# A mixture-of-experts stage: one copy moved to another engine, a group of transposes issued later, two slots exchanged

## The chip, the cores and the metric

The kernel runs on one core of a Trainium2 chip. The metric is the device time of one execution in microseconds (us), the median of several runs. TensorE (PE in the rows) multiplies matrices into the eight PSUM banks; ScalarE (ACT) and VectorE (DVE) copy results out of PSUM and convert data; GpSimd (POOL) issues the gathers and scattered stores, SyncE (SP) the loads of weights. Each engine works through its own instruction list in the order of the program, and waits on semaphores for the others.

## What is computed

Attention with capped scores, a dense layer with a normalisation, and then a routed layer: each of 1792 tokens is sent to one of 8 experts, and the expert's two weight matrices are applied with a ReLU between them. The change lies in this last layer:

```python
def _moe2_ref(x, modality_id, w_gate, modality_bias, w1, w2):
    logits = x @ w_gate + modality_bias[modality_id]
    e_idx = np.argmax(logits, axis=1)
    ...
    for e in range(E):
        mask = e_idx == e
        if not mask.any():
            continue
        h = np.maximum(x[mask] @ w1[e], 0.0)          # 768 -> 1024
        out[mask] = gate_w[mask, None] * (h @ w2[e])  # 1024 -> 768
```

## The kernel before

Attention, the dense layer and the routing fill the first 545 us. Then two tiles of tokens of an early expert (names with `e_`) are finished, and the tokens that are left go through *slots* of fixed size in the order of `STATIC`, each with one expert's weights: kind D holds 512 tokens, F 256, H 128. The order before is D0, H0, D1, H1, F0. Two small slots of 32 tokens (kind T) ride along, T0 with D0 and T1 with D1 (`SMALL`). The gathered rows of tokens are `yg`.

For each slot the program writes the same stages, and the order in which `run_slots` writes them is the order in which every engine does them:

- `s_tr` of the *next* slot: TensorE transposes its token tiles, six 128x128 blocks a tile, into PSUM (`xt`), three blocks to a half; ScalarE copies each half to `xh`, VectorE writes what the rounding left over to `xl`.
- `s_h` (D, F) or `s_hh` (H): the first matrix. The accumulators are `ph`: eight PSUM banks for D, four for F, two for H. Each product is made of three matmuls, high by high, high by low and low by high. For D and F, ScalarE's ReLU gives `hh` and VectorE's remainder `hl`. For H the result lies the other way round, so ScalarE writes `hu`, `s_ht` transposes it (`ht`), and then come `hh` and `hl`.
- `s_o`: the second matrix, accumulators `po`, eight blocks of weights (f = 0 to 7). `store` scales the result into `ob` (half on ScalarE, half on VectorE), and GpSimd scatters it to the output. The last slot does its tiles one after the other.
- A T slot has its own stages: `t_tr` (rows of the small slot are scaled on VectorE, transposed into `tp`, copied to `tx` on ScalarE), `t_h` (`th`, ReLU to `tu`), `t_ht` (transposed into `tt`, copied to `hT`), `t_o` (`to`, copied to `tb`). In lines L1191 to L1193 the copy of `tt` to `hT` is VectorE's:

```python
        pt = ctile(f"tt{sname(s)}")[:, :NC1]
        ...
        dve.tensor_copy(h, pt)
```

All of these PSUM tiles come from one pool of eight banks (`ctile`): a new tile takes the bank that was given back longest ago, and its first matmul waits until that bank's last reader is done.

Weights arrive by `c_load` (SyncE loads a block into one of four `raw` buffers) and `c_split` (ScalarE casts it to `wh`, L1025; VectorE writes `wl`, L1026, which gives the raw buffer back). Six blocks of 512 KB belong to a slot's first matrix, eight of 384 KB to its second. They go into two rings of buffers, 12 and 16 tiles, so that a block can be split only when the block that had its place is used up. `step`, called ahead of each block of matmuls, writes the splits that this block needs and up to `QUOTA` = 2 more. So splits stand in ScalarE's and VectorE's lists between the copies of the slots.

Of the kernel before, what the change touches and what calls it, by code (L numbers as in the profile page):

```python
# [15 lines left out]
ALU = mybir.AluOpType  # L16
# [4 lines left out]
B, H, S, D = 4, 12, 448, 64  # L21
NT, DM, DF, NE = 1792, 768, 1024, 8
# [4 lines left out]
NF = DF // P  # L27
# [15 lines left out]
TAIL = (12, 12, 10)  # L43
NS = NK * len(KINDS)
NG = COL0["T"]
STATIC = [("D", 0), ("H", 0), ("D", 1), ("H", 1), ("F", 0)]
SMALL = {0: ("T", 0), 2: ("T", 1)}
PLAIN = 3
DIRECT = 6
# [41 lines left out]
def attn_moe_kernel(ctx, tc, qt, kt, vv, cap, w_in, w_out, g_ln, ids, w_gate, mbias, w1, w2, out):  # L91
    nc = tc.nc
    pe, act, dve, pool, sp = nc.tensor, nc.scalar, nc.vector, nc.gpsimd, nc.sync
# [5 lines left out]

    keys = ["rest", ("E", 0), ("E", 1)] + [(x, i) for x in STATIC + list(SMALL.values()) for i in range(UNIT[x[0]])]  # L100
    oviews = dict(zip(keys, dram_disjoint_views(out, len(keys))))

    def oview(s, i):
        return oviews.get((s, i), oviews["rest"])
# [83 lines left out]
    def route_consts(tp):  # L188
# [39 lines left out]
        for i, kind in enumerate(KINDS):  # L228
            pool.memset(ck[:, i:i + 1], float(COL0[kind]))
            there = [x for x in STATIC + list(SMALL.values()) if x[0] == kind]  # L230
            pool.memset(own[:, i:i + 1], float(UNIT[kind] * len(there)))
# [623 lines left out]
    t = (B - 1) * S // P - 1  # L855
# [101 lines left out]
    while msteps or due:  # L957
        if msteps:
            msteps.pop(0)[1]()
        if outs and outs[-1] in groups:  # L960
            g = outs[-1]
# [22 lines left out]
    ss = {}  # L984
    NC1, NC2 = DF // 4, DM // 4

    def ctile(nm):
        return late["ps"].tile([P, 512], F32, tag="C", name=nm)

    def sname(s):  # L990
        return f"{s[0]}{s[1]}"

    def cols(s):
        kind, i = s
        return [COL0[kind] + UNIT[kind] * i + x for x in range(UNIT[kind])]
# [41 lines left out]
            gs.append(g)  # L1037
        ss[s] = {"g": gs, "ga": ga}

    def s_tr(s, part=range(4)):  # L1040
        nm = sname(s)
        n = len(cols(s))
        if 0 in part:
            ss[s]["xh"] = g2.tile([P, ND, n * P], F32R, tag="xh2", name=f"xh2_{nm}")
            ss[s]["xl"] = g2.tile([P, ND, n * P], F32R, tag="xl2", name=f"xl2_{nm}")
        xh, xl, ga = ss[s]["xh"], ss[s]["xl"], ss[s]["ga"]
        for i in range(n):
            if i not in part:
                continue
            g = ss[s]["g"][i]  # L1050
            o = slice(i * P, (i + 1) * P)
            for q in range(2):
                pt = ctile(f"xt{nm}_{i}_{q}").rearrange("p (b c) -> p b c", c=P)
                r = slice(3 * q, 3 * q + 3)
                for d in range(3):
                    pe.transpose(pt[:, d, :], g[:, (3 * q + d) * P:(3 * q + d + 1) * P], ident)
                act.copy(xh[:, r, o], pt[:, :3, :])
                dve.tensor_sub(xl[:, r, o], pt[:, :3, :], xh[:, r, o])
            dve.tensor_scalar(ga[:, i:i + 1], g[:, DM:DM + 1], 1e-9, None, op0=ALU.add)
        if n - 1 in part:  # L1060
            dve.reciprocal(ga[:, :n], ga[:, :n])

    def s_h(s, step):
# [53 lines left out]
            dve.tensor_sub(hl[:, c, :], pt, hh[:, c, :])  # L1117
        ss[s]["hh"], ss[s]["hl"] = hh, hl

    def s_o(s, step, last):  # L1120

        nm = sname(s)
        hh, hl, ga = ss[s]["hh"], ss[s]["hl"], ss[s]["ga"]
        cs = cols(s)
        pos = [[ctile(f"po{nm}_{i}_{hf}") for hf in range(2)] for i in range(len(cs))]
        ws = {}

        def store(i):
            ob = g2.tile([P, DM], F32, tag="tm", name=f"ob{nm}_{i}", bufs=NTM)
            act.activation(ob[:, :HD], pos[i][0][:, :HD], AF.Copy, scale=ga[:, i:i + 1])  # L1130
            dve.tensor_scalar(ob[:, HD:], pos[i][1][:, :HD], ga[:, i:i + 1], None, op0=ALU.mult)
            pool.indirect_dma_start(out=oview(s, i), out_offset=IndirectOffsetOnAxis(ap=sidx[:, cs[i]:cs[i] + 1], axis=0),
                                    in_=ob, in_offset=None, bounds_check=NT, oob_is_err=False)

        for group in [[i] for i in range(len(cs))] if last else [list(range(len(cs)))]:
            for f in range(NF):
                if f not in ws:
                    step(s, 1, f)
                    ws[f] = ss.pop((s, 1, f))
                wh, wl = ws[f]  # L1140
                for i in group:
                    o = slice(i * P, (i + 1) * P)
                    for hf in range(2):
                        c = slice(hf * HD, (hf + 1) * HD)
                        p = pos[i][hf][:, :HD]
                        pe.matmul(p, hh[:, f, o], wh[:, c], start=(f == 0), stop=False)  # L1146
                        pe.matmul(p, hh[:, f, o], wl[:, c], start=False, stop=False)  # L1147
                        pe.matmul(p, hl[:, f, o], wh[:, c], start=False, stop=(f == NF - 1))  # L1148
                    if f == NF - 1:
                        store(i)  # L1150
# [3 lines left out]
    def t_gather(s):  # L1154
        g = g2.tile([P, YW], F32, tag="gT", name=f"yg{sname(s)}")[:TT]
        pool.indirect_dma_start(out=g, out_offset=None, in_=ysc,
                                in_offset=IndirectOffsetOnAxis(ap=gidxT[:TT, s[1]:s[1] + 1], axis=0),
                                bounds_check=NT, oob_is_err=False)
        ga = g2.tile([TT, 1], F32, tag="gt", name=f"gt{sname(s)}", bufs=2)
        ss[s] = {"g": g, "ga": ga}  # L1160

    def t_tr(s):
        g, ga = ss[s]["g"], ss[s]["ga"]
        dve.tensor_scalar(ga, g[:, DM:DM + 1], 1e-9, None, op0=ALU.add)
        dve.reciprocal(ga, ga)
        dve.tensor_scalar(g[:, :DM], g[:, :DM], ga, None, op0=ALU.mult)
        x = g2.tile([P, DM], F32, tag="tm", name=f"tx{sname(s)}", bufs=NTM)[:, :ND * TT].rearrange("p (b c) -> p b c", c=TT)
        pt = ctile(f"tp{sname(s)}")[:, :ND * TT].rearrange("p (b c) -> p b c", c=TT)
        for d in range(ND):
            pe.transpose(pt[:, d, :], g[:, d * P:(d + 1) * P], ident[:TT, :TT])  # L1170
        act.copy(x, pt)
        ss[s]["x"] = x
# [14 lines left out]
    def t_ht(s):  # L1187
        u = ss[s]["u"]
        pt = ctile(f"tt{sname(s)}")[:, :NC1]
        for b in range(NC1 // P):  # L1190
            pe.transpose(pt[:, b * P:(b + 1) * P], u[:, b * P:(b + 1) * P], ident)  # L1191
        h = g2.tile([P, DM], F32, tag="tm", name=f"hT{sname(s)}", bufs=NTM)[:, :NC1]
        dve.tensor_copy(h, pt)  # L1193
        ss[s]["h"] = h

    def t_o(s, step):
# [15 lines left out]
    def run_slots(seq, small, lead=None):  # L1212

        smalls = [small[n] for n in sorted(small)]
        use = []
        for n, s in enumerate(seq):
            t = [small[n]] if n in small else []
# [42 lines left out]

        if seq[0][0] == "T":
            t_gather(seq[0])
            t_tr(seq[0])
            t_h(seq[0], step)
            t_ht(seq[0])
            t_o(seq[0], step)
            return

        def first(i):
            if i < len(cols(seq[0])):  # L1270
                s_tr(seq[0], (i,))
            elif smalls:
                t_tr(smalls[0])
                if smalls[1:]:
                    t_gather(smalls[1])
# [13 lines left out]
        for n, s in enumerate(seq):  # L1289
            nx = seq[n + 1] if n + 1 < len(seq) else None  # L1290
            t, tn = small.get(n), small.get(n + 1)
            (s_hh if s[0] == "H" else s_h)(s, step)
            if t:
                t_h(t, step)
            if s[0] != "H":
                if nx:
                    s_tr(nx)
            else:
                if nx:
                    s_tr(nx, (0,))  # L1300
                s_ht(s)
                if nx:
                    s_tr(nx, (1, 2, 3))
            if t:
                t_ht(t)
            if tn:
                t_tr(tn)
                for x in smalls[smalls.index(tn) + 1:][:1]:
                    t_gather(x)
            if n + 2 < len(seq):  # L1310
                s_gather(seq[n + 2])
            if t:
                t_o(t, step)
            s_o(s, step, n == len(seq) - 1)

    def lead(advance, tr):

# [13 lines left out]
    with tc.manual_schedule():  # L1331
        run_slots(STATIC, SMALL, lead)

# [3 lines left out]
    def rest(kind, n, i):  # L1337
        if i == MAXS[kind]:
            return
        with tc.If(n > UNIT[kind] * i):  # L1340
            if kind == "T":
                run_slots([(kind, i)], {0: (kind, i)})
            else:
                run_slots([(kind, i)], {})
            rest(kind, n, i + 1)

    with tc.If(more > 0):
        for i, kind in enumerate(KINDS):
            n = nc.values_load(nsl[0:1, i:i + 1], min_val=0, max_val=UNIT[kind] * NK)
            rest(kind, n, len([x for x in STATIC + list(SMALL.values()) if x[0] == kind]))  # L1350
    for pl_ in (late["ps"], late["g1"], g2, g3, g4):
# [40 lines left out]
```

## Time and profile before

| | |
|---|---|
| median of 3 runs | 815.36 us (812.24 to 815.41) |
| the profiled execution: its own time | 816.4 us |
| its span, first to last instruction | 814.6 us |
| TensorE busy, share of the span | 95% |
| mean granted TensorE clock | 0.97 |

The profile is of one execution, which is 1.0 us above the median. A row of a timeline gives start, duration, engine, line, operation, output and inputs, the count of merged instructions and, in brackets, the engine's idle time before it with what ended it. Durations of consecutive matmuls overlap, so that their cost is the distance of their starts.

### The profile page before, as it was taken

The numbers are of one execution on the slowest core, as the hardware profiler recorded it, in microseconds if no ns is written. First come the engines' busy times: TensorE is split into PE (matmuls) and PEld (weight loads), VectorE is DVE, ScalarE is ACT, GpSimd is POOL, SyncE is SP. The second block draws the span as 40 slices with busy tenths as digits, with TensorE's granted clock in tenths as the row PEclk, the third lists the DMA queues.
The fourth block names the chain that finished last, engine by engine and source line by source line (L and its number), as shares of the span: only waits on it lengthen the run. The fifth ranks groups of instructions, "written<-read, shape, count | busy, mean of one in ns | idle before, by whom it ended". The sixth has DMA issues, their size and how long they took to land.

```text
span 814.6 us, 11543 instructions
## 1 busy us (share of the span) xinstructions
PE 770.6 (95%) x4158; PEld 593.0 (73%) x4158; DVE 478.4 (59%) x843; ACT 389.8 (48%) x539; POOL 260.1 (32%) x325
## 2 busy tenths in 40 slices
PE   7888989999999999999999999899999989999983
PEld 2324545676677877577769799799879978799982
DVE  4999897757764566675435755756146171461730
ACT  5665853766755545656651224434144252442530
POOL 3763244544443342438623213441200101001000
PEclk9979979999999999999999999999999989999997
DMA  7866532123322222223000302467928259382711
GB/s 187 253 190 188 175 110 55 47 76 99 97 70 65 77 57 76 88 63 94 12 20 20 138 20 97 153 229 245 387 81 258 104 201 394 130 259 103 239 66 42
DMA packets 41206, 107.28 MB, mean 132 GB/s; under 512 B 7047, under 2 KB 18833, under 8 KB 41138
## 3 DMA queue, kind: packets, MB, share of 16 engines
q1 hardware_dynamic: 34610, 77.01, 29.8%
q0 software_dynamic: 6528, 29.42, 10.4%
q8 instruction: 35, 0.57, 0.3%
q14 instruction: 33, 0.27, 0.1%
HBM read 95.33 MB, written 11.27 MB: 131 GB/s over the span
## 4 chain that ended last, share of the span: by engine, by line
PE 79%; DVE 9%; DMA 5%; issue 3%; ACT 2%; SPq 1%; POOL 0%; POOLq 0%; DVEq 0%; ACTq 0%
PE av L710 8%; PE h L540 5%; PE y L590 5%; PE h L542 5%; PE y L591 5%; PE h L541 5%; PE y L592 5%; PE sc L684 4%; PE sc L686 4%; PE poD L1146 3%; PE poD L1148 3%; PE poD L1147 3%; PE phD L1080 3%; PE phD L1081 3%; PE phD L1079 3%
## 5 line engine op out<-in xcount | busy, mean ns | idle before, releaser
L688 ACT ACTIVATE e<-sc,sc 112x896 f32<-112x896 f32 x96 | 95.8, 1005 | 81.9 <-PE sc L686 67.5
L689 ACT ACTIVATE e<-e,cap_t 112x896 f32<-112x896 f32 x96 | 99.1, 1043 | 1.2
L710 PE MATMUL av<-e,v 112*64 112x448 f32 x384 | 97.4, 577 | 1.9 <-ACT e L689 1.0
L590 PE MATMUL y<-wouh,lh 128*128 128x388 f32 x224 | 77.6, 346 | 1.8 <-ACT lh L580 1.8
L592 PE MATMUL y<-wouh,ll 128*128 128x388 f32 x224 | 76.1, 340 | 0.3 <-DVE ll L581 0.2
L591 PE MATMUL y<-woul,lh 128*128 128x388 f32 x224 | 76.0, 339 | 0.0
L540 PE MATMUL h<-winh,xh 128*128 128x512 f32 x168 | 69.4, 413 | 0.2
L684 PE MATMUL sc<-qs,kh 128*112 128x448 f32 x168 | 64.7, 385 | 4.3 <-DVE qs L668 3.0
L542 PE MATMUL h<-winh,xl 128*128 128x512 f32 x168 | 66.7, 397 | 0.2 <-DVE xl L528 0.2
L541 PE MATMUL h<-winl,xh 128*128 128x512 f32 x168 | 66.3, 395 | 0.0
L686 PE MATMUL sc<-qs,kl 128*112 128x448 f32 x168 | 62.8, 374 | 0.0
L710 PEld LDWEIGHTS av<-e,v 112*64 112x64 f32 x384 | 26.3, 140 | 45.9 <-issue 36.5
L699 POOL TENSOR_TENSOR es<-es,et 112x448 f32<-112x448 f32 x36 | 45.4, 1263 | 28.0 <-DVE et L698 27.1
L669 POOL TENSOR_TENSOR kl<-kr,kh 128x448 fp32r<-128x448 f32 x28 | 34.5, 1232 | 52.8 <-PE sc L686 20.1
L590 PEld LDWEIGHTS y<-wouh,lh 128*128 128x128 f32 x224 | 42.1, 188 | 12.1 <-issue 7.9
L1026 DVE TENSOR_TENSOR wl_H<-raw_H,wh_H 128x768 fp32r<-128x768 f32 (+1 forms) x28 | 29.1, 1070 | 36.9 <-ACT wh_H L1025 36.9
L540 PEld LDWEIGHTS h<-winh,xh 128*128 128x128 f32 x168 | 31.6, 188 | 18.9 <-issue 10.7
L1026 DVE TENSOR_TENSOR wl_D<-raw_D,wh_D 128x768 fp32r<-128x768 f32 (+1 forms) x28 | 29.9, 1071 | 24.9 <-ACT wh_D L1025 23.5
L668 DVE TENSOR_TENSOR qs<-qr,qs 64x448 fp32r<-64x448 f32 x42 | 39.2, 934 | 6.5 <-ACT qs L667 5.3
L1146 PE MATMUL poD<-wh_D,hhD 128*128 128x384 f32 x128 | 43.0, 336 | 0.0
L1148 PE MATMUL poD<-wh_D,hlD 128*128 128x384 f32 x128 | 42.8, 334 | 0.0
L1147 PE MATMUL poD<-wl_D,hhD 128*128 128x384 f32 x128 | 42.8, 334 | 0.0
(392 smaller groups left out, 1811.5 us busy)
## 6 DMA issues: line engine op xcount, KB each, us to landing
kr<-in_kt_dram SPq DMA_DIRECT2D x92, 112.0 KB, 2.5
qr<-in_qt_dram SPq DMA_DIRECT2D x88, 112.0 KB, 2.9
rawi<-in_w_in_dram POOLq DMA_DIRECT2D x12, 512.0 KB, 4.8
rawo<-in_w_out_dram POOLq DMA_DIRECT2D x16, 384.0 KB, 4.0
raw_D<-in_w_dram SPq DMA_DIRECT2D x12, 512.0 KB, 3.6
wr_T<-in_w_dram SPq DMA_DIRECT2D x16, 384.0 KB, 4.1
raw_D<-in_w_dram SPq DMA_DIRECT2D x16, 384.0 KB, 4.8
wr_T<-in_w_dram SPq DMA_DIRECT2D x12, 512.0 KB
```

The source lines that it names most:

```text
L540: pe.matmul(o, s["xh"][d], winh[d][:, c], start=(d == 0), stop=False)
L541: pe.matmul(o, s["xh"][d], winl[d][:, c], start=False, stop=False)
L542: pe.matmul(o, s["xl"][d], winh[d][:, c], start=False, stop=(d == ND - 1))
L590: pe.matmul(o, s["lh"][f], wouh[f][:, c], start=(f == 0), stop=False)
L591: pe.matmul(o, s["lh"][f], woul[f][:, c], start=False, stop=False)
L592: pe.matmul(o, s["ll"][f], wouh[f][:, c], start=False, stop=(f == NF - 1))
L684: pe.matmul(ps[:CK, c, :S], kh[:, k0:k0 + CK], qs, start=True, stop=plain(b, p))
L686: pe.matmul(ps[:CK, c, :S], kl[:, k0:k0 + CK], qs, start=False, stop=True)
L688: act.activation(e, ps[:CK, :, :S], AF.Tanh, scale=sc8[:CK])
L689: act.activation(e, e, AF.Exp, scale=cap_t[:CK])
L710: pe.matmul(o[64 * j:64 * j + 64, :S], v[:, 2 * cp + c, 64 * j:64 * j + 64], et[b, p, j, cp][:, c, :], start=(cp == 0 and c == 0), stop=(c ...
L1146: pe.matmul(p, hh[:, f, o], wh[:, c], start=(f == 0), stop=False)
```

## The change

Three edits. The copy of `tt` to `hT` goes from VectorE to ScalarE, and in the D slots `t_ht` is written between the two halves of the next slot's first tile. `t_tr` is split: the scaling (`t_sc`, VectorE) stays where it was, and the transposes and their copy, which for T1 stood ahead of H0's second matrix, are written inside it, ahead of its block f = 5. And F0 comes before H1.

```diff
-STATIC = [("D", 0), ("H", 0), ("D", 1), ("H", 1), ("F", 0)]
+STATIC = [("D", 0), ("H", 0), ("D", 1), ("F", 0), ("H", 1)]
...
-    def s_tr(s, part=range(4)):
+    def s_tr(s, part=range(4), halves=(0, 1)):
...
-            for q in range(2):
+            for q in halves:
...
-    def s_o(s, step, last):
+    def s_o(s, step, last, late_=None):
...
             for f in range(NF):
+                if f == NF - 3 and late_:
+                    late_()
                 if f not in ws:
                     step(s, 1, f)
...
-    def t_tr(s):
+    def t_sc(s):
         g, ga = ss[s]["g"], ss[s]["ga"]
         dve.tensor_scalar(ga, g[:, DM:DM + 1], 1e-9, None, op0=ALU.add)
         dve.reciprocal(ga, ga)
         dve.tensor_scalar(g[:, :DM], g[:, :DM], ga, None, op0=ALU.mult)
+
+    def t_tr(s):
+        g = ss[s]["g"]
...
-        dve.tensor_copy(h, pt)
+        act.copy(h, pt)
...
-            if s[0] != "H":
-                if nx:
-                    s_tr(nx)
-            else:
+            if s[0] == "H":
                 if nx:
                     s_tr(nx, (0,))
                 s_ht(s)
                 if nx:
                     s_tr(nx, (1, 2, 3))
-            if t:
+            elif t:
+                s_tr(nx, (0,), (0,))
                 t_ht(t)
+                s_tr(nx, (0,), (1,))
+                s_tr(nx, (1, 2, 3))
+            elif nx:
+                s_tr(nx)
             if tn:
-                t_tr(tn)
+                t_sc(tn)
...
-            s_o(s, step, n == len(seq) - 1)
+            s_o(s, step, n == len(seq) - 1, (lambda: t_tr(tn)) if tn else None)
```

**Place 1, slot H0.** TensorE's list from the last transposes of D1's tokens (`xtD1`) to H0's second matrix (`poH0`), and further on the first matmul of three of D1's eight accumulators (`phD1`). What a row waits for stands in brackets (Activation is ScalarE). Before:

```order
L1056 MATMUL xtD1_3_1_6039<-ident_61,ygD1_3_5585 128x128 x2
L1170 MATMUL tpT1_6051<-ident_61,ygT1_5228 128x32 [waits DMASW1_49,DVE_49,PE_49]
L1170 MATMUL tpT1_6051<-ident_61,ygT1_5228 128x32 x5
L1146 MATMUL poH0_0_0_6064<-wh1_H0_0_5787,hhH0_5991 128x384 [waits PE_49,Activation_49]
...
L1079 MATMUL phD1_5_6180<-xh2_D1_5976,wh0_D1_0_6101 128x512 [waits PE_49]
L1079 MATMUL phD1_6_6181<-xh2_D1_5976,wh0_D1_0_6101 128x512 [waits Activation_49]
L1079 MATMUL phD1_7_6182<-xh2_D1_5976,wh0_D1_0_6101 128x512 [waits DVE_49]
```

Of the change:

```order
L1056 MATMUL xtD1_3_1_6039<-ident_61,ygD1_3_5585 128x128 x2
L1149 MATMUL poH0_0_0_6059<-wh1_H0_0_5787,hhH0_5991 128x384 [waits DVE_49]
...
L1151 MATMUL poH0_0_1_6060<-wh1_H0_4_5859,hlH0_5992 128x384
L1176 MATMUL tpT1_6145<-ident_61,ygT1_5228 128x32 [waits DMASW1_49,DVE_49,PE_49]
L1176 MATMUL tpT1_6145<-ident_61,ygT1_5228 128x32 x5
L1149 MATMUL poH0_0_0_6059<-wh1_H0_5_6072,hhH0_5991 128x384 [waits Activation_49]
...
L1080 MATMUL phD1_5_6184<-xh2_D1_5976,wh0_D1_0_6096 128x512 [waits Activation_49]
L1080 MATMUL phD1_6_6185<-xh2_D1_5976,wh0_D1_0_6096 128x512 [waits Activation_49]
L1080 MATMUL phD1_7_6186<-xh2_D1_5976,wh0_D1_0_6096 128x512 [waits DVE_49]
```

`tpT1` has moved from ahead of all 48 `poH0` matmuls to behind the thirtieth. Three of D1's accumulators take the banks of `tpT1` and of the two `poH0`; the first matmul of `phD1_5`, which had waited for nothing but TensorE itself, now waits for ScalarE.

**The same place on ScalarE.** `txT1` is the copy that gives `tpT1`'s bank back, `obH0` the one that gives back the first of `poH0`; `wh1_H0` are the last casts of H0's second matrix, `wh0_D1` those of D1's first. Before:

```order
L1057 CAST xh2_D1_5976<-xtD1_3_1_6039 128x3x128 [waits PE_49]
L1171 COPY txT1_6050<-tpT1_6051 128x192 [waits DVE_49,DMASW2_49,PE_49,Activation_49]
L1025 CAST wh1_H0_5_6077<-raw1_H0_5_5821 128x768 [waits DMAHW1_49]
...
L1025 CAST wh0_D1_3_6129<-raw0_D1_3_6099 128x1024 [waits DMAHW7_49]
L1025 CAST wh0_D1_4_6133<-raw0_D1_4_6111 128x1024 [waits DMAHW0_49]
L1130 ACTIVATE obH0_0_6167<-poH0_0_0_6064,gaH0_5267 128x384 [waits DVE_49,DMASW3_49,PE_49,Activation_49]
L1025 CAST wh0_D1_5_6183<-raw0_D1_5_6117 128x1024 [waits DMAHW1_49]
```

Of the change:

```order
L1057 CAST xh2_D1_5976<-xtD1_3_1_6039 128x3x128 [waits PE_49]
L1025 CAST wh1_H0_5_6072<-raw1_H0_5_5821 128x768 [waits DMAHW1_49,DVE_49]
...
L1025 CAST wh0_D1_3_6124<-raw0_D1_3_6094 128x1024 [waits DMAHW7_49]
L1025 CAST wh0_D1_4_6128<-raw0_D1_4_6106 128x1024 [waits DMAHW0_49]
L1177 COPY txT1_6144<-tpT1_6145 128x192 [waits DVE_49,DMASW2_49,PE_49,Activation_49]
L1131 ACTIVATE obH0_0_6171<-poH0_0_0_6059,gaH0_5267 128x384 [waits DVE_49,DMASW3_49,PE_49,Activation_49]
L1025 CAST wh0_D1_5_6187<-raw0_D1_5_6112 128x1024 [waits DMAHW1_49]
```

`txT1` has moved behind three casts of H0 and five of D1. `obH0` still stands behind the same casts.

**Place 2, slot F0 on ScalarE.** `hhF0` is the ReLU of F0's first matrix; the casts ahead of it are those written by `step` during that matrix. Before:

```order
L1025 CAST wh1_F0_5_7145<-raw1_F0_5_7079 128x768 [waits DMAHW1_49,DVE_49]
L1025 CAST wh1_F0_6_7149<-raw1_F0_6_7109 128x768 [waits DMAHW2_49,DVE_49]
L1025 CAST wh1_F0_7_7177<-raw1_F0_7_7115 128x768 [waits DMAHW3_49,DVE_49,PE_49]
L1084 ACTIVATE hhF0_7031<-phF0_0_7033 128x512 [waits PE_49,Activation_49]
L1084 ACTIVATE hhF0_7031<-phF0_1_7034 128x512 [waits PE_49]
```

Of the change:

```order
L1025 CAST wh1_F0_7_6898<-raw1_F0_7_6767 128x768 [waits DMAHW4_49,DVE_49]
L1025 CAST wh0_H1_0_6904<-raw0_H1_0_6860 128x1024 [waits DMAHW5_49,DVE_49,PE_49]
L1025 CAST wh0_H1_1_6934<-raw0_H1_1_6866 128x1024 [waits DMAHW6_49,PE_49]
L1025 CAST wh0_H1_2_6964<-raw0_H1_2_6896 128x1024 [waits DMAHW7_49,PE_49]
L1025 CAST wh0_H1_3_6994<-raw0_H1_3_6902 128x1024 [waits DMAHW0_49,PE_49]
L1085 ACTIVATE hhF0_6845<-phF0_0_6847 128x512 [waits PE_49]
L1085 ACTIVATE hhF0_6845<-phF0_1_6848 128x512 [waits PE_49]
```

Before, all eight casts of F0's own second matrix stood ahead of `hhF0` in this stage. Now F0's last three come at the stage's start, and the casts just ahead of `hhF0` are H1's, each waiting for a block of F0 to be used up.

## Rows read from the trace of the kernel before

**Rows 1.** The page, part 1: busy time of each engine.

```profile
PE 770.6 (95%) x4158; PEld 593.0 (73%) x4158; DVE 478.4 (59%) x843; ACT 389.8 (48%) x539; POOL 260.1 (32%) x325
```

**Rows 2.** All waits of TensorE, 598 to 801 us: total, times, longest.

```profile
PE tpT L1170 <- issue: 4.0, 1, 4.0
PE toT L1204 <- DVE hTT L1193: 3.4, 2, 1.7
PE poF L1146 <- ACT hhF L1084: 1.7, 1, 1.7
PE poF L1148 <- DVE hlF L1085: 0.5, 1, 0.5
PE poH L1148 <- DVE hlH L1117: 0.2, 1, 0.2
```

**Rows 3.** Stretches: length; PE, PEld, DVE, ACT, POOL busy (instructions); PEclk; DMA share, GB/s.

```profile
649.30:657.70 8.40, 4.44 (x39) 4.12 (x37) 6.21 (x18) 4.79 (x12) 1.04 (x1) 0.90 0.17 47
657.70:668.50 10.80, 10.80 (x50) 10.80 (x50) 6.81 (x7) 6.95 (x9) 0.00 (x0) 0.76 0.69 237
668.50:701.20 32.70, 32.70 (x145) 26.81 (x143) 12.62 (x15) 10.63 (x15) 3.30 (x3) 1.00 0.94 360
...
709.50:742.90 33.40, 33.40 (x197) 33.40 (x194) 16.34 (x17) 14.72 (x19) 2.24 (x3) 1.00 0.54 174
...
779.50:800.00 20.50, 18.30 (x96) 17.95 (x96) 5.15 (x8) 3.65 (x8) 0.98 (x1) 0.92 0.06 22
```

**Rows 4.** Chain that ended last, 601 to 607 us, slot T0.

```profile
602.82 0.49 ACT xh_H L1057
...
603.33 1.02 DVE xl_H L1058 x2
...
604.52 0.43 DVE hTT L1193
```

**Rows 5.** Timeline of TensorE, slot H0.

```profile
650.87 2.13 PE L1056 MATMUL xtD<-ident,ygD 128*128 128x128 f32 x18
656.96 0.82 PE L1170 MATMUL tpT<-ident,ygT 32*128 32x32 f32 x6 [3.96 <-issue]
...
668.47 0.40 PE L1079 MATMUL phD<-xh_D,wh_D 128*128 128x512 f32 x1
```

**Rows 6.** Timeline of VectorE, slot H0.

```profile
656.25 0.61 DVE L1166 TENSOR_SCALAR ygT<-ygT,gtT 32x768 f32<-32x768 f32 x1
658.93 2.69 DVE L1026 TENSOR_TENSOR wl_H<-raw_H,wh_H 128x768 fp32r<-128x768 f32 x3 [2.08 <-ACT wh_H L1025]
...
661.55 1.22 DVE L1026 TENSOR_TENSOR wl_D<-raw_D,wh_D 128x1024 fp32r<-128x1024 f32 x1
```

**Rows 7.** Timeline of ScalarE, slot H0.

```profile
648.86 1.28 ACT L1103 ACTIVATE huH<-phH 128x512 f32<-128x512 f32 x2 [7.42 <-PE phH L1101]
...
650.76 1.11 ACT L1116 CAST hhH<-htH 128x512 fp32r<-128x512 f32 x2
...
657.85 0.32 ACT L1171 COPY txT<-tpT 128x192 f32<-128x192 f32 x1 [3.68 <-issue]
...
668.16 1.06 ACT L1025 CAST wh_D<-raw_D 128x1024 fp32r<-128x1024 f32 x1 [0.22 <-DMA raw_D<-in_w_dram]
669.12 0.57 ACT L1130 ACTIVATE obH<-poH,gaH 128x384 f32<-128x384 f32 x1
```

**Rows 8.** Issue of the load of D1's block 4, timeline of SyncE.

```profile
662.79 0.33 SPq L1012 DMA_DIRECT2D raw_D<-in_w_dram  x1
```

**Rows 9.** Loads of `raw_D`, 600 to 700 us, from issue to landing.

```profile
DMA to landing us min/median/max: 3.6/4.0/10.3
```

**Rows 10.** Chain that ended last, 779 to 783 us, slot F0.

```profile
779.88 0.84 ACT wh_F L1025
...
781.70 0.61 DVE hlF L1085
```

**Rows 11.** Timeline of TensorE, its last matmul.

```profile
800.10 0.34 PE L1148 MATMUL poF<-wh_F,hlF 128*128 128x384 f32 x1
```

More of the change, by code (lines that the diff above doesn't have):

```diff
@@ L1038, in s_gather @@
         ss[s] = {"g": gs, "ga": ga}
-    def s_tr(s, part=range(4)):
+    def s_tr(s, part=range(4), halves=(0, 1)):
         nm = sname(s)
         n = len(cols(s))
-        if 0 in part:
+        if 0 in part and 0 in halves:
             ss[s]["xh"] = g2.tile([P, ND, n * P], F32R, tag="xh2", name=f"xh2_{nm}")
@@ L1058, in s_tr @@
                 dve.tensor_sub(xl[:, r, o], pt[:, :3, :], xh[:, r, o])
-            dve.tensor_scalar(ga[:, i:i + 1], g[:, DM:DM + 1], 1e-9, None, op0=ALU.add)
-        if n - 1 in part:
+            if 1 in halves:
+                dve.tensor_scalar(ga[:, i:i + 1], g[:, DM:DM + 1], 1e-9, None, op0=ALU.add)
+        if n - 1 in part and 1 in halves:
             dve.reciprocal(ga[:, :n], ga[:, :n])
@@ L1262, in run_slots @@
             t_gather(seq[0])
+            t_sc(seq[0])
             t_tr(seq[0])
@@ L1272, in first @@
             elif smalls:
+                t_sc(smalls[0])
                 t_tr(smalls[0])
```

## The prediction

> **What bounds the kernel now.** I read the page first: TensorE is busy for 95% of the span [rows 1], so time can come only from its waits and from a lower clock. Next came the list of all TensorE waits in the stretch that the change touches, and it is short: 9.8 us in six places [rows 2]. The reader should see that three of the four names with real time in them (`tpT`, `toT`, `poF`) are ones that the diff moves. Then the table of stretches, to see what the waits cost besides: after the 4.0 us ahead of `tpT`, the 48 `poH` matmuls took 10.80 us at a granted clock of 0.76, and the 96 `poF` took 20.50 us at 0.92 [rows 3]. At full clock 192 matmuls of the same shape took 33.40 us, 0.174 us each (the stretch from 709.5 to 742.9 [rows 3]), so the 48 should take 8.35: the slower of the clock's two levels (1.2 and 2.4 GHz) cost 2.45 us there. For F0, from 779.5 to the last start at 800.10 [rows 11] are 20.6 us, 95 steps of 0.174 are 16.5, and of the 4.1 left 2.2 are the two waits [rows 2]: 1.9 us of clock. The chain that ended last and the timelines then say who was late. I assume that what follows the last matmul (14.5 us to the end of the span) stays: the last store is one tile in both.
>
> The sum is made against the profiled execution, 816.4 us, 1.0 above the median of 815.36.
>
> **T0 and T1, the copy of `tt`.** In T0 ScalarE ends the first `xh_H` at 603.30; VectorE then does two `xl_H` (1.02), two tiny operations and the copy `hTT` at 604.52 for 0.43 [rows 4], and `toT` starts near 605.0 after a wait of 1.7 [rows 2]. In the change the copy stands on ScalarE right behind that first `xh_H`. Its cost there is not in the trace: a 128x192 copy took 0.32 [rows 7] and a 128x384 one 0.49 [rows 4]; I take 0.4. So `toT` starts at about 603.75, and T0 gains 1.25 (1.15 to 1.35). In T1 the next slot is now F0 with two tiles; nine transposes at 0.12 (18 in 2.13 [rows 5]) stand between `tt` and `toT` and fill the rest. Six of them are work that lay in H1's stage before, so nothing is added: T1 gains 1.6. VectorE loses the copy and has nothing behind it that TensorE awaits.
>
> **H0, the later transposes of T1.** Before, TensorE ended D1's transposes at 653.0, waited 3.96 for VectorE's scaling of `ygT` (done at 656.86 [rows 6]), and came to `phD` at 668.47 [rows 5]. In the change `poH` follows at 653.0: its `hh` and `hl` are made ahead of most of D1's remainders. Add 48 times 0.174 and `tpT` at 0.6 (0.82 at the slow clock is the upper bound [rows 5], nothing the lower), and `phD` is reached at 661.95, 6.5 us earlier. The last three blocks of `wl_H` are in time: VectorE starts them at 656.86 instead of 658.93 [rows 6], one each 0.9 us, done at 657.8, 658.7 and 659.6; they are due at 658.8, 659.9 and 660.9.
>
> But something is late next. `phD` is eight banks, and its sixth accumulator takes the bank that `txT` gives back. `txT` now stands on ScalarE behind the cast of D1's block 4, and that cast waits for its load. The load can be issued when VectorE has done `wl_D` of block 0: before, 661.55 + 1.22 = 662.77, issued at 662.79 [rows 6, 8], landed just ahead of the cast at 668.16 [rows 7], 5.3 us later. In the change block 0 ends 2.0 us earlier, near 660.8, since VectorE comes to these blocks 2.07 us sooner; so the load lands at 666.1 and the cast ends at 667.2, `txT` at 667.5, `obH` on ScalarE at 668.1, and VectorE's half, behind its own 1.22 for block 4, at 669.1. TensorE wants the sixth bank 15 matmuls after 661.95; at 32.70/144 = 0.227 each [rows 3] that is 665.35. It waits 2.2 us for `txT`, then about 0.35 for VectorE's half of `obH` at the eighth bank. Bounds: nothing if the load lands in the shortest 3.6 [rows 9] and the rest of the casts run ahead; 7.5 if it takes the longest, 10.3. I take 2.55, by the load itself.
>
> Does the clock fall in such a wait? A wait of 4.0 cost 2.45, one of 1.7 with 0.5 behind it 1.9, while the one of 1.7 ahead of T1's `toT` is followed by a stretch at 1.00 [rows 2, 3]. At 2.2 in one piece I count a fall, at 1.9 (0 to 2.45). H0 is left with 6.5 - 2.55 - 1.9 = 2.05.
>
> That ScalarE keeps its order is seen in the row of `txT`: idle for 3.68 ahead of it, and the casts of `wh_H`, whose blocks had long landed, came only behind it [rows 7]. The Trainium skill says so too, page PSUM — Partial Sum Buffer, section Engine vs sequencer instructions: the queues of ScalarE, VectorE and GpSimd are strictly first in, first out. It is a rule that speaks against moving `tpT` late, as the trace does; by it the time is 807, and were casts overtaken it would be the first rival's 802.7.
>
> **F0 ahead of H1.** Before, F0 came last, and its weights arrived as they were used: the last `wh_F` ran from 779.88 to 780.72, when F0's first matrix was over at 779.5, and `hhF` and `hlF` (at 781.70) came behind it in the lists [rows 10]. That is the 4.1 us above. In the change F0's weights are split during D1's 33 us of second matrix, as H1's were, and the casts ahead of `hhF` are H1's. The latest of them waits for F0's fourth block, two blocks ahead of the end: with six blocks in 17.4 us that is 5.8 us, against 1.06 + 1.22 for the split. `hhF` is on time, and the transposes of H1 cover the ReLU's tail: 4.1 gained.
>
> H1 now ends the program, with no next slot to transpose. From the last `phH`: the second ReLU ends 0.8 later and both take 1.28, `hh` 0.56 each [rows 7], `hl` about 0.65 (0.61 in [rows 10]), so the first matmul with `hl` can start some 2.1 us after `phH`, over 8 transposes and 2 matmuls, 1.2 us. TensorE waits 0.9 in pieces instead of 0.2 [rows 2]: 0.7 lost (0 to 2.6, if the clock fell too).
>
> **Sum.** 1.25 + 1.6 + 2.05 + 4.1 - 0.7 = 8.3. The profiled execution would be 808.1, the median 807.1.
>
> **Rivals.**
> *No wait for banks.* If D1's loads come sooner (H0's casts need no longer wait for `txT`), the 2.55 and the 1.9 fall away: 802.7. For it: DMA was at 47 GB/s ahead of these loads [rows 3]; against it: the load waits for VectorE, whose list has only 2 us less. 0.20.
> *The clock falls at H1 as well.* The waits there come in three or four pieces within 2 us; as after F0's two waits, 1.9 more: 809.0. Against it: T1's wait of 1.7 cost none. 0.15. The Trainium skill, page TensorE: Matmul & The Clock Gate, section A second HAM failure mode: psum-queue depth-cycling, tells of a kernel whose many short idle spells between groups of matmuls made the clock swing; by that rule the time is this rival's 809.0, and no row here shows it for waits below 1 us.
> *The gain goes into the load.* With a landing of 10.3 [rows 9] the wait for banks grows by 5.0 and the clock costs another 1.9: 807.1 + 6.9 = 814.0, no change. 0.10.
> *The edit at F0 does nothing.* If `hhF` is still late, because H1's casts wait for raw blocks as F0's did, the 4.1 stay: 811.2. 0.05.
> *Slower.* The same place at H0: the accumulator waits behind a cast, the cast behind a load. To end above 819.5 in the median the bank wait must grow by 12.4, with 1.9 of that from the clock: the load of block 4 would have to take about 15.8 us. No row has that. 0.05.
>
> **How the numbers follow.** The forecast, with or without its fall of the clock (807.1 or 805.2), has 0.45, the rivals 0.20, 0.15, 0.10, 0.05 and 0.05. A change of this kernel below 0.5%, 4.1 us, cannot be told from none; so faster means below 811.3. Forecast and the first two rivals are faster, 0.80, and of the 0.15 of the next two, which lie at 811 to 814, I count 0.06: 0.86; same 0.09, slower 0.05. The range goes from 802.0, just below the first rival, to 811.5, above the clock's rival and the idle edit; it leaves out the load's rival and slower, and a little at the low end.
>
> **What would show it.** `toT` starts within 0.5 us of its inputs in T0 and without a wait in T1. `tpT` has no wait, and `poH` runs at full clock. `phD` waits about 2.5 us within its first block, released by ScalarE's `txT` or `obH`, with D1's block 4 cast just before. `poF` no longer waits for `hhF`, and near the end `htH` and `poH` wait some 0.9 us together. The prediction is wrong if `phD` starts without a wait, if that wait is above 5 us, or if F0 or H1 waits for a cast of its weights.

## The result, and the profile after

The changed kernel takes 807.3 us (median of 5 runs, 806.01 to 808.86) against 815.36 (5 runs, 812.24 to 816.69): a ratio of 0.9908, 95% interval 0.9882 to 0.9934. In a second set of runs, beside the experiments, it took 806.07 (6 runs) against 816.27 (17 runs): 0.9885, 0.9855 to 0.9915. The forecast was 807.1. The profiled execution took 806.09 us with a span of 804.4; its page, part 1, beside [rows 1]:

```profile
PE 766.8 (95%) x4158; PEld 587.3 (73%) x4158; DVE 477.9 (59%) x841; ACT 390.8 (49%) x541; POOL 259.4 (32%) x325
```

TensorE's busy time fell by 3.8 us with the same 4158 instructions: fewer of them ran at the lower clock (the mean granted is 0.977 instead of 0.97). The rest is in the waits. The list of all its waits from 590 to 806 us, beside the five lines of [rows 2], has one line:

```profile
PE phD L1080 <- ACT txT L1177: 1.9, 1, 1.9
```

The waits for `tpT`, `toT`, `hhF` and `hlF` are gone, and the one that the prediction expected has come, at D1's accumulators. TensorE's timeline around it, beside [rows 5], and its last matmul, beside [rows 11]:

```profile
657.00 0.55 PE L1176 MATMUL tpT<-ident,ygT 32*128 32x32 f32 x6
...
660.74 0.40 PE L1080 MATMUL phD<-xh_D,wh_D 128*128 128x512 f32 x1
...
666.25 0.50 PE L1080 MATMUL phD<-xh_D,wh_D 128*128 128x512 f32 x1 [1.90 <-ACT txT L1177]
...
667.51 0.40 PE L1082 MATMUL phD<-xh_D,wl_D 128*128 128x512 f32 x1
667.82 0.51 PE L1080 MATMUL phD<-xh_D,wh_D 128*128 128x512 f32 x1
...
789.63 0.34 PE L1151 MATMUL poH<-wh_H,hlH 128*128 128x384 f32 x1
```

`tpT` has no wait now. 15 matmuls after 660.74 the sixth accumulator stops for 1.90; at the eighth (667.82) the step from the matmul ahead is 0.31 instead of 0.23, a trace of the wait for VectorE's half of `obH`, which ends at 667.76. Who was late is seen in three short pieces: VectorE's remainder of D1's block 0 (and that half of `obH`), SyncE's issue of block 4's load, and ScalarE's casts of D1 with what stands behind them (beside [rows 6 to 8]).

```profile
658.26 1.21 DVE L1026 TENSOR_TENSOR wl_D<-raw_D,wh_D 128x1024 fp32r<-128x1024 f32 x1
...
667.15 0.61 DVE L1132 TENSOR_SCALAR obH<-poH,gaH 128x384 f32<-128x384 f32 x1
```
```profile
659.49 0.33 SPq L1012 DMA_DIRECT2D raw_D<-in_w_dram  x1
```
```profile
660.24 1.05 ACT L1025 CAST wh_D<-raw_D 128x1024 fp32r<-128x1024 f32 x1 [4.09 <-DMA raw_D<-in_w_dram]
661.94 1.05 ACT L1025 CAST wh_D<-raw_D 128x1024 fp32r<-128x1024 f32 x1 [0.66 <-DMA raw_D<-in_w_dram]
663.64 1.05 ACT L1025 CAST wh_D<-raw_D 128x1024 fp32r<-128x1024 f32 x1 [0.65 <-DMA raw_D<-in_w_dram]
664.93 1.04 ACT L1025 CAST wh_D<-raw_D 128x1024 fp32r<-128x1024 f32 x1 [0.24 <-DMA raw_D<-in_w_dram]
665.88 0.31 ACT L1177 COPY txT<-tpT 128x192 f32<-128x192 f32 x1
666.09 0.59 ACT L1131 ACTIVATE obH<-poH,gaH 128x384 f32<-128x384 f32 x1
```

The remainder ends at 659.47, the load is issued at 659.49, its cast starts at 664.93, 5.4 us later, and `txT` at 665.88, when the last `tpT` transposes had been done for 8 us. ScalarE itself was idle for 4.09 us ahead of the first cast shown. The prediction named block 4's load alone, but it is the last of four: the casts of blocks 1 to 4 each waited for their own load (4.09, 0.66, 0.65 and 0.24 us). Had only block 4's load come sooner, its cast could by these rows have begun some 0.24 us sooner, right behind block 3's (an estimate). The table of stretches, with the columns of [rows 3]: H0's last 18 `poH` with `tpT`, D1's first matrix, F0's second matrix, and the end of H1:

```profile
657.00:660.74 3.74, 3.74 (x25) 3.70 (x25) 2.46 (x3) 0.50 (x1) 0.00 (x0) 1.00 0.92 269
660.74:695.90 35.16, 33.26 (x145) 26.69 (x144) 15.61 (x17) 13.85 (x19) 2.25 (x2) 1.00 0.97 368
754.50:771.20 16.70, 16.70 (x99) 16.70 (x98) 10.61 (x15) 8.61 (x13) 0.00 (x0) 1.00 0.46 143
779.50:790.50 11.00, 10.33 (x57) 9.07 (x56) 3.69 (x5) 3.93 (x7) 0.00 (x0) 1.00 0.01 3
```

The clock is at 1.00 in all four, also behind the wait of 1.90: the fall that the prediction had counted did not come in this execution.

To set the runs against each other without the first 590 us, which the change leaves alone, this table has the distances between TensorE's landmarks: the first matmul of T0's first matrix (`th`), the first `ph` of H0, of D1, the first `th` of T1, the first `ph` of the slot behind it, and the last matmul of the program. Differences of starts in the timelines, in us.

| run | T0 | H0 | D1 | T1 | last two slots | sum |
|---|---|---|---|---|---|---|
| before | 41.63 | 27.34 | 32.77 | 41.63 | 57.23 | 200.60 |
| changed | 40.33 | 20.74 | 35.19 | 40.79 | 52.91 | 189.96 |
| before, second profile | 41.62 | 27.67 | 32.78 | 41.63 | 56.69 | 200.39 |
| changed, second profile | 40.33 | 20.75 | 36.67 | 40.78 | 52.94 | 191.47 |
| changed, third profile | 40.33 | 20.75 | 36.68 | 40.80 | 52.95 | 191.51 |
| changed, fourth profile | 40.33 | 20.75 | 36.73 | 40.80 | 52.92 | 191.53 |
| edit 1 alone | 40.33 | 27.77 | 32.78 | 40.33 | 55.32 | 196.53 |
| edit 2 alone | 41.63 | 20.75 | 34.78 | 41.63 | 55.37 | 194.16 |
| edit 3 alone | 41.62 | 26.24 | 32.78 | 42.64 | 52.91 | 196.19 |
| casts behind `txT` | 40.33 | 20.75 | 32.78 | 40.80 | 52.92 | 187.58 |
| one more cast ahead of `txT` | 40.34 | 20.74 | 36.48 | 40.80 | 52.93 | 191.29 |
| the same, second profile | 40.33 | 20.75 | 37.77 | 40.81 | 52.94 | 192.60 |
| before, F0's casts later | 41.63 | 27.78 | 32.78 | 41.62 | 52.98 | 196.79 |
| casts behind, F0 last | 40.34 | 20.74 | 32.78 | 40.34 | 52.96 | 187.16 |

Of the 10.64 us between the first two rows, 0.17 are lost ahead of T0 and some 0.2 behind the last matmul (14.7 us to the span's end instead of 14.5), which leaves the 10.2 between the spans. The medians differ by 8.1: the profiled execution of before lies 1.0 above its median, that of the change 1.2 below. Each row is one execution, and two of its columns vary where the edits change nothing: before's place at H0 took 26.24 to 27.78 in five profiles, and its place at F0 57.23 and 56.69, but 55.32 and 55.37 with edit 1 or edit 2 alone. In both places the stage is longer where the clock stayed low for longer (the last section and the experiments on the clock come back to this).

### The profile page after: what moved, and what is told of

Its sections match the earlier page's. It is cut to its first block, busy times and chain, and to the rows that moved or that the text cites. A ratio compares the mean times of both kernels' runs of the same rounds, so it can differ in the third digit from the quotient of the medians.

```text
span 804.4 us, 11556 instructions
## 1 busy us (share of the span) xinstructions
PE 766.8 (95%) x4158; PEld 587.3 (73%) x4158; DVE 477.9 (59%) x841; ACT 390.8 (49%) x541; POOL 259.4 (32%) x325
## 4 chain that ended last, share of the span: by engine, by line
PE 75%; DVE 6%; issue 4%; DMA 1%; ACT 1%; POOL 0%; POOLq 0%; SPq 0%; ACTq 0%; DVEq 0%
PE av L710 7%; PE h L540 5%; PE y L590 5%; PE h L542 5%; PE y L591 5%; PE h L541 5%; PE y L592 5%; PE sc L684 3%; PE sc L686 3%; PE poD L1149 3%; PE poD L1151 3%; PE poD L1150 3%; PE phD L1080 3%; PE phD L1081 3%; PE phD L1082 3%
```

## The experiments

**Each edit alone.** Theory: the gain is the sum of three separate things. Rival: one edit carries it, or two pay only together.

Edit 1 (the copy on ScalarE between the half tiles; the transposes of T1 and the slots as before):

```diff
-        dve.tensor_copy(h, pt)
+        act.copy(h, pt)
...
+            elif t:
+                s_tr(nx, (0,), (0,))
                 t_ht(t)
+                s_tr(nx, (0,), (1,))
+                s_tr(nx, (1, 2, 3))
```

> Only the first edit: ScalarE copies tt to hT, t_ht between the halves; slots and the transposes of T1 as before. By my theory (each of the three edits removes its own wait, and they add up) toT starts 1.3 us sooner in T0 and in T1, and nothing later gives it back: 2.6 us less than before. By the rival (TensorE only waits for the same weights or banks a little later) the waits of toT fall from 1.7 to about 0.4 and the time stays within 0.5 us.

Measured: 812.05 us (12 runs) against 815.93 (25 runs), ratio 0.9963 (0.9942 to 0.9985). TensorE's waits:

```profile
PE tpT L1176 <- issue: 4.0, 1, 4.0
PE poF L1149 <- ACT hhF L1085: 1.3, 1, 1.3
PE poF L1151 <- DVE hlF L1086: 0.5, 1, 0.5
PE poH L1151 <- DVE hlH L1118: 0.2, 1, 0.2
```

Both waits for `toT` are gone, and T0 and T1 are 1.30 shorter each. One thing was not expected: the waits at F0 stand (1.3 and 0.5), but the clock did not fall behind them. F0's second matrix from the first start to the last (columns of [rows 3]), of before and then of edit 1 alone:

```profile
781.26:800.10 18.84, 18.37 (x96) 18.04 (x96) 3.45 (x6) 2.14 (x5) 0.98 (x1) 0.91 0.06 23
```
```profile
779.45:796.77 17.32, 16.84 (x95) 16.52 (x96) 3.45 (x6) 2.13 (x5) 0.98 (x1) 1.00 0.07 25
```

Edit 2 (the transposes of T1 inside H0's second matrix):

```diff
             if tn:
-                t_tr(tn)
+                t_sc(tn)
...
-            s_o(s, step, n == len(seq) - 1)
+            s_o(s, step, n == len(seq) - 1, (lambda: t_tr(tn)) if tn else None)
```

> Only the second edit: T1's transposes inside H0's second matrix. My theory: tpT without a wait, phD of D1 6.6 us sooner, then a wait of 1.9 to 2.5 us in its first block for txT, so that D1's first matrix ends 4.0 to 4.5 us sooner than before; 4.2 us less in all, 2.4 if the clock falls in that wait. Rival (the wait for txT comes from the slot order, as F0's loads replace H1's): no wait at phD, 6.6 us less.

Measured: 810.45 us (8 runs), ratio 0.9945 (0.9921 to 0.9968). `tpT` has no wait, and the wait for banks is there without the other edits, 1.5 us:

```profile
PE toT L1210 <- DVE hTT L1199: 3.4, 2, 1.7
PE phD L1080 <- ACT txT L1177: 1.5, 1, 1.5
PE poF L1149 <- ACT hhF L1085: 1.4, 1, 1.4
PE poF L1151 <- DVE hlF L1086: 0.5, 1, 0.5
PE poH L1151 <- DVE hlH L1118: 0.2, 1, 0.2
```

So it does not come from the order of the slots, which is that of before here. It is shorter than the 1.9 to 2.5 that were expected; why is not shown. H0 and D1 together take 55.53 instead of 60.11: 4.6 gained.

Edit 3 (F0 ahead of H1, nothing else):

```diff
-STATIC = [("D", 0), ("H", 0), ("D", 1), ("H", 1), ("F", 0)]
+STATIC = [("D", 0), ("H", 0), ("D", 1), ("F", 0), ("H", 1)]
```

> Only the third edit: F0 ahead of H1. My theory: the waits of poF (1.7 and 0.5) and the lower clock behind them go, H1's end waits some 0.9 us: 3.4 us less than before. Rival (any last slot gets its weights late): the time stays, and htH or poH of H1 waits for casts of its weights, 3 us or more.

Measured: 812.49 us (12 runs), ratio 0.9961 (0.9943 to 0.998). The last two slots take 52.91 instead of 57.23; T1 loses 1.01: F0's twelve transposes stand ahead of `tt` instead of H1's six, and the wait for `toT` there is 2.0 instead of 1.7. Net 3.3. By the table, with each edit counted in the stages that it touches, the three are worth 2.6, 4.6 and 3.3, 10.5 together, and the whole gave 10.64. By the ratios it is 3.0, 4.5 and 3.2 against 7.5 and 9.4 for the whole, each with an interval of some 2 us to either side. Each edit gains by itself, and the parts add up within what can be measured. The 3.3 of edit 3 is counted from a profile of before in which the clock fell at F0: from the 55.3 of edits 1 and 2, where it did not, only 1.4 are left.

**The wait for banks.** The prediction put it down to `txT` standing behind the cast of D1's block 4. If so, it goes when the casts stand behind `txT`, and it grows with one more ahead. `QH` has, for an H slot's first and second matrix, the number of last blocks at which `step` writes no splits beyond those that are due. A larger second number leaves fewer casts of D1 ahead of `txT`, which is written ahead of block 5: one instead of five here.

```diff
-QH = (6, 4)
+QH = (6, 6)
```

> The changed kernel with QH = (6, 6): step writes the extra casts in an H slot's second matrix only up to block 1, so that txT and obH stand behind one cast of D1 and no longer behind five. My theory (phD waits for its bank because txT stands behind the cast of D1's block 4, which waits for its load): no wait in phD, D1's first matrix ends 2.2 to 2.4 us sooner than in the changed kernel, 805.0 where that gives 807.3. Rival (the bank wait only hides that D1's weights are late): phD waits 1.5 us or more at block 1 or 2 for wh_D or wl_D instead, same time as the changed kernel.

Measured: 803.35 us (802.79 to 804.11, 5 runs), ratio 0.9846 (0.9821 to 0.9872). TensorE has no wait in the list from 590 us on. ScalarE now gives the banks back at once, and D1's first matrix is back at the length of [rows 3]:

```profile
658.09 0.32 ACT L1177 COPY txT<-tpT 128x192 f32<-128x192 f32 x1 [1.47 <-issue]
660.92 0.58 ACT L1131 ACTIVATE obH<-poH,gaH 128x384 f32<-128x384 f32 x1 [2.51 <-PE poH L1151]
661.40 1.99 ACT L1025 CAST wh_D<-raw_D 128x1024 fp32r<-128x1024 f32 x2
```
```profile
661.20:693.95 32.75, 32.75 (x145) 26.84 (x144) 15.72 (x17) 13.89 (x18) 2.81 (x2) 1.00 1.00 380
```

D1 falls from 35.19 to 32.78, and no weight is late for it. All 5 runs lie below all 5 and 6 of the changed kernel (lowest 804.4), though the 6 were taken on another chip; the 2.4 us at D1, or 3.9 against its profiles with a fall of the clock, are where the gain is seen.

```diff
-QH = (6, 4)
+QH = (6, 3)
```

> The changed kernel with one more cast of D1 (that of block 5) ahead of txT and obH in ScalarE's list. Theory (the accumulator waits for txT, txT behind a cast, the cast behind a load): the wait of 1.9 us at the sixth accumulator grows by the 1 to 2.5 us by which block 5 is ready later than block 4, to 3 to 4.5 us, and the time by as much, 1.5 to 3 us over the changed kernel; 2 to 3 us more if the clock falls, as it did after the wait of 4.0 us. Rival (the wait is not due to the casts, but to TensorE coming to D1 too early for the banks): the wait stays at 1.9 us and the time within 0.5 us of the changed kernel.

Measured: 808.23 us (806.82 to 809.88, 6 runs) against 806.07 (804.4 to 809.38) of the changed kernel on the same chip, 2.2 more, with runs that overlap; the trace tells more. ScalarE and TensorE:

```profile
665.98 1.04 ACT L1025 CAST wh_D<-raw_D 128x1024 fp32r<-128x1024 f32 x1 [0.35 <-DMA raw_D<-in_w_dram]
666.93 0.31 ACT L1177 COPY txT<-tpT 128x192 f32<-128x192 f32 x1
```
```profile
667.29 0.50 PE L1080 MATMUL phD<-xh_D,wh_D 128*128 128x512 f32 x1 [3.19 <-ACT txT L1177]
667.63 0.39 PE L1081 MATMUL phD<-xl_D,wh_D 128*128 128x512 f32 x1
667.86 0.40 PE L1082 MATMUL phD<-xh_D,wl_D 128*128 128x512 f32 x1
```

One cast more, and the wait grows from 1.9 to 3.2, with `txT` 1.1 later and D1 longer by 1.29. The theory holds in both directions; the rival, that TensorE simply comes too early, would have kept 1.9 in the one and in the other.

**Does the clock fall behind that wait?** In the first profile of the change it did not, where the prediction had charged 1.9 us for it. So a second execution of the same kernel was profiled.

> The changed kernel itself, a second time, beside the variants of it that follow. It should give the 807.3 us of its first runs within 1.5 us, and its trace one wait of TensorE behind T0, of 1.5 to 2.5 us, at the sixth accumulator of D1 for the copy txT. If that wait is absent in this execution, or is followed by a fall of the clock, what the first profile showed there holds for one execution only.

Measured: 806.07 us (804.4 to 809.38, 6 runs). The wait is 2.0 in this profile, and now the clock falls. TensorE behind the wait:

```profile
666.24 0.50 PE L1080 MATMUL phD<-xh_D,wh_D 128*128 128x512 f32 x1 [1.98 <-ACT txT L1177]
...
667.06 0.63 PE L1080 MATMUL phD<-xh_D,wh_D 128*128 128x512 f32 x1
667.49 0.63 PE L1081 MATMUL phD<-xl_D,wh_D 128*128 128x512 f32 x1
...
670.45 0.39 PE L1082 MATMUL phD<-xh_D,wl_D 128*128 128x512 f32 x1
```

From 667.06 to 670.05 the steps are 0.43 instead of 0.23: the lower of the two levels. D1 takes 36.67, 1.48 more than in the first profile, of which 0.08 is the longer wait. Four single executions more, two of them of the changed kernel:

> The changed kernel, a third profile, to see how often the clock falls behind the wait at the sixth accumulator (so far in one of two). If the wait's length decides (1.9 us no fall, 2.0 us a fall), a wait of 2.0 us or more is followed by a stretch of D1 at a clock below 1.00, a shorter one is not. Rival (the same wait falls in some executions and not in others, whatever its length): falls and waits don't go together.

> The changed kernel, a fourth profile, with the same two theories as the third.

> The kernel with block 5's cast ahead of txT as well, a second profile; in the first a wait of 3.2 us was not followed by a fall. If the wait's length decides, it is not now either, or the first one was an exception; by the rival a fall behind about 3.2 us can be seen here.

> The kernel before, a second profile. In the first the clock fell behind F0's waits of 1.7 and 0.5 us; with only edit 1 and with only edit 2, which leave F0 alone, it did not. If the fall there comes in some executions only, F0's second matrix takes either 18.8 us from first to last start, as in the first profile, or 17.3 us, as in those two.

Measured: 806.96, 808.24, 811.72 and 815.44 us. D1's first matrix in the two of the changed kernel, then in the one with the extra cast:

```profile
660.43:696.75 36.32, 34.32 (x144) 27.90 (x144) 15.29 (x17) 13.55 (x19) 2.25 (x2) 0.95 0.94 358
```
```profile
661.72:698.10 36.38, 34.34 (x144) 27.93 (x144) 15.29 (x17) 13.40 (x19) 2.25 (x2) 0.95 0.93 355
```
```profile
664.21:701.95 37.74, 34.64 (x145) 27.91 (x144) 15.71 (x17) 13.85 (x19) 2.06 (x2) 0.95 0.90 342
```

The waits are 2.0, 2.0 and 3.1, and the clock falls in all three; in the extra cast's first profile a wait of 3.2 had no fall. In the second profile of before F0's waits are 1.1 and 0.5, and the clock falls in its second matrix:

```profile
PE poF L1146 <- ACT hhF L1084: 1.1, 1, 1.1
PE poF L1148 <- DVE hlF L1085: 0.5, 1, 0.5
```
```profile
780.52:799.45 18.93, 18.45 (x96) 18.13 (x96) 3.45 (x6) 2.14 (x5) 0.98 (x1) 0.91 0.06 24
```

With edit 1 or 2 alone, waits of 1.3 or 1.4 and 0.5 had none. So the length of the wait alone does not decide it: the changed kernel had the fall in 3 of 4 profiles, the kernel before at F0 in 2 of 2, and longer waits were spared. What decides is open. At F0 the order of lists is that of before in edits 1 and 2 too, so that place had the fall in 2 of 4 profiles. The fall costs about 1.4 us here.

**Is it the exchange of the slots, or the order of the casts?** The prediction's reason for F0 was that `hhF` stood behind the casts of its own last blocks. Then F0 can stay last, if only these casts stand behind `hhF`. First in the kernel before. For an F slot, `step` now writes no extra splits at the last three blocks of a matrix, instead of at the last one alone, so the casts of F0's last three blocks come behind `hhF`:

```diff
-                                       and k < (ND, NF)[w] - (QH[w] if s[0] == "H" else 1)):
+                                       and k < (ND, NF)[w] - (QH[w] if s[0] == "H" else 3 if s[0] == "F" else 1)):
```

> The kernel before, F0 still last, with one number changed: the casts of F0's last three blocks are written behind hhF instead of ahead of it. Theory (F0 lost time by the order in ScalarE's and VectorE's lists, not by the weights' arrival): the waits of 1.7 and 0.5 us for hhF and hlF are gone, the casts of these blocks are in time for their matmuls, and the time is 1.5 to 4 us below the kernel before, as far as the clock had fallen there. Rival (the weights of the last slot are late in any order): TensorE waits for wh_F at one of the last three blocks instead, about 2 us in all, and the time is that of the kernel before within 1 us.

Measured: 812.63 us (12 runs) against 816.27, ratio 0.996 (0.9942 to 0.9978): the gain of the exchange alone (0.9961). No wait for `hhF`, `hlF` or a cast of F0's weights is in the list. ScalarE, and TensorE's first `poF`:

```profile
777.69 0.83 ACT L1025 CAST wh_F<-raw_F 128x768 fp32r<-128x768 f32 x1 [1.41 <-DMA raw_F<-in_w_dram]
778.43 2.63 ACT L1084 ACTIVATE hhF<-phF 128x512 fp32r<-128x512 f32 x4
780.95 2.29 ACT L1025 CAST wh_F<-raw_F 128x768 fp32r<-128x768 f32 x3
```
```profile
780.14 0.28 PE L1081 MATMUL phF<-xh_F,wl_F 128*128 128x256 f32 x1
780.26 0.33 PE L1146 MATMUL poF<-wh_F,hhF 128*128 128x384 f32 x1
```

`hhF` runs while `ph` is still being computed, and `poF` follows without a gap. The weights of the last slot are not late; the rival falls. Then edits 1 and 2 with all casts in their better places and F0 last, against the changed kernel:

```diff
-STATIC = [("D", 0), ("H", 0), ("D", 1), ("F", 0), ("H", 1)]
+STATIC = [("D", 0), ("H", 0), ("D", 1), ("H", 1), ("F", 0)]
...
-                                       and k < (ND, NF)[w] - (QH[w] if s[0] == "H" else 1)):
+                                       and k < (ND, NF)[w] - (6 if s == ("H", 0) else QH[w] if s[0] == "H" else 3 if s[0] == "F" else 1)):
```

> Edits 1 and 2 of the change with the casts behind txT and obH in H0, but the slots in the order of before (H1, then F0 last), and F0's last three casts behind hhF. Theory (the exchange of the slots helps only by the order of the casts): the exchange isn't needed, no wait for hhF, and the time is that of the best kernel so far, 803.4 us, within 1 us, with at most 0.9 us gained at the end, where no H slot waits for its second ReLU. Rival (the exchange gives something of its own, since T1 has no transposes of F0 to cover its copy and F0's weights come last): 805 to 807 us, with a wait for toT of T1 or for wh_F.

Measured: 803.21 us (802.32 to 806.63, 6 runs), ratio 0.9854 (0.9825 to 0.9882), the same as with F0 ahead and the casts behind `txT`. In the table it is 0.42 shorter: T1, without six of F0's transposes, by 0.46, while the last two slots, which now hold them, take as long as before (52.96 against 52.92), since the waits at H1's end do not arise. Beyond the order of the casts, the exchange of the slots has no worth that these runs show.

## Why the prediction was right

The waits went and came where the prediction put them: `tpT`, `toT` and `hhF` wait no longer, and D1's sixth accumulator waits for `txT`. That the median came within 0.2 us of the 807.1 is in part luck: the second set of runs has 806.07, the clock's term was too large, and D1 alone differs by 1.5 us from one execution of the changed kernel to the next.

**Edit 1.** T0: 1.25 forecast, 1.30 in the table; the copy took 0.37 and 0.38 on ScalarE, against 0.4. T1: 1.6 forecast, with F0's transposes moved into the stage. T1 shows only 0.84, but it holds six transposes more, 0.72 at 0.12 each, which the last two slots are rid of: 1.56.

**H0.** 6.5 forecast up to `phD`, 6.6 measured between the two profiles (5.5 to 7.0 against the five profiles that have before's order there). The wait for banks came where it was put, behind the cast of block 4 and its load: forecast 2.2 and 0.35, while D1 grew by 2.4 with 1.9 in the named wait. The load took 5.4 from issue to cast, 5.3 forecast; what the prediction had too simple is that all four loads set this time, not block 4's alone (0.24 of ScalarE's waits). Moving the casts removes it, adding one makes it longer, so this chain is shown. The Trainium skill, page PSUM — Partial Sum Buffer, section Engine vs sequencer instructions, has the queue strictly first in, first out; the trace agrees: the transposes for `txT` were done at 657.55, ScalarE had nothing to do until 660.24, and `txT` still ran only at 665.88, behind the casts.

**The clock.** This is the term that was mis-sized: 1.9 for a fall behind that wait. In the execution first profiled it cost nothing; in three others of the same kernel it came and cost 1.4. The prediction allowed for 0 to 2.45, but took 1.9 as if a fall were certain. H0 and D1 together took 60.11 before, 55.93 without the fall and 57.42 with it: H0 is worth 4.2 or 2.7, where 2.05 was forecast. At F0 the fall was also charged with 1.9; the second matrix with the fall and without it, 18.84 before and 17.32 with edit 1 alone, differ by 1.5. Most of the other 0.4 is in the first steps, which are longer than 0.174 with edit 1 as well: 17.32 less 16.5 for the 95 steps and 0.5 for the wait for `hlF` leaves 0.3.

**F0 and H1.** 4.1 - 0.7 = 3.4 forecast. The last two slots gained 4.32, of which 0.72 are the transposes that T1 took over: 3.6. Against profiles of before's order without the fall at F0 (55.32, 55.37) it would be 1.7. The first matmul with `hl` started 2.2 us behind the last `phH` start plus its step (779.27 to 781.72, less 0.23), 2.1 forecast. Its eight transposes and two matmuls take 1.3 of that, so the waits come to the 0.9 forecast, in pieces that the list of waits doesn't name. No fall of the clock followed; the rival that the clock falls at H1 did not occur in four profiles (52.91 to 52.95 for the last two slots). The Trainium skill, page TensorE: Matmul & The Clock Gate, section A second HAM failure mode: psum-queue depth-cycling, tells of a kernel in which frequent short idle spells between groups of matmuls made the clock swing; the few waits below 1 us at H1's end showed none of it here. What the experiments add is that the gain at F0 belonged to the order of casts, as the prediction argued, and not to the slots' order.

With these sizes the sum is 1.3 + 1.56 + 2.7 + 3.6 = 9.2 with the fall at D1, 10.6 without; the forecast said 8.3. Against an execution of before without its fall at F0 it is some 1.9 less (57.23 - 55.32). The measured ratios give 7.5 and 9.4 (0.0092 of 815.36, 0.0115 of 816.27), within that spread. The first rival, no wait for banks, gave 802.7, and 803.35 was measured once the casts stand behind `txT`; but its reason was that D1's loads come sooner, and there the bank is free because `txT` waits for no load.

## What to carry to other kernels

Before a copy that frees a PSUM bank is moved later in an engine's list, look at what then stands ahead of it: a cast that waits for a load passes the load's time on to the next accumulator that takes the bank, and casts whose blocks are needed later belong behind such a copy. When a stage seems to suffer from its place among the stages, change the order of the lists inside it first; here a limit on how far casts run ahead gave all that the exchange of two slots gave. A term for a fall of the clock is to be entered as a chance, and more than one profile is needed to judge it.

## What the hardware showed unexpectedly

The clock's fall is not the same from one execution of a kernel to the next. Waits of 2.0 us ahead of the sixth accumulator were followed by the lower level in three profiles, and those of 1.5 (edit 2 alone) and 1.9 in one each were not; of the two with 3.1 and 3.2 only the shorter was. Behind the wait of 4.0 for `tpT` the lower level came in all five profiles that have it, but not for the same time: the stage H0 took from 26.24 us (edit 3 alone) to 27.78 (before, F0's casts later), though neither changes that place and the wait was 4.0 in all.
